# Stage A's stores on ScalarE's queue, back tables ahead of the filter copies, less filler: the set-up of an FFT and gated-FFN kernel

**Chip, cores, metric.** One core of one Trainium2 chip. The metric is the device time of a whole execution in microseconds (us). The traces' spans, from the first to the last instruction, are mostly some 1.8 us shorter than these times.

## The reference, cut to what matters

```python
def _attn_ref(x, filt_r, filt_i):            # x: 8 x 3008 x 256, f32
    X = np.fft.rfft(x, axis=1)
    Y = X * (filt_r + 1j * filt_i)[None]     # filters: 1505 x 256
    return np.fft.irfft(Y, n=x.shape[1], axis=1)

def _moe_ref(x, w_gate, w_val, w_out):       # on 24064 x 256 rows, d_ff 1536
    return np.maximum(x @ w_gate, 0.0) * (x @ w_val) @ w_out
```

The transform of 3008 is done as 94 x 32 with matmuls. For batch 0 nothing can hide it: its x is loaded, multiplied by a 94-point matrix ("stage A", `psA`), stored to a scratch in DRAM (`Abuf`), read back in another layout (`at`), and only then goes through the second transform, the products with the filters, and the inverse. The other seven batches do this beside the gated FFN, which keeps TensorE busy for the rest of the time.

## The kernel before: the parts concerned

Stage A of one batch: 16 tiles `psA`, cast by ACT to `asb`, and one store to `Abuf` for every four (there are four such quarters `c`):

```python
def items_a(b):
    def one(c, j, st):
        ...
        nc.tensor.matmul(psA[0:NROW], WA, XF[c * NC2 // NX2][:, o:o + 512], start=True, stop=True)
        nc.scalar.copy(dst, psA[0:NROW])
        if j == 3:
            eng = nc.scalar if b and c > 1 else nc.sync
            eng.dma_start(_ap(Abuf[b], ...), st["asb"][:NROW])
```

The set-up (cut). `load_x` issues 15 loads on SP (SyncE), three for each group of columns; GpSimd (POOL) loads the filters once the first half of x has landed; `warm(n)` is n filler matmuls on `junk`, meant to keep TensorE's clock up:

```python
    load_x(0, nc.sync, ((0, 0, q), (0, q, 2 * q), (0, 2 * q, 4 * q), (1, 0, 2 * q), (1, 2 * q, 4 * q)))
    nc.sync.dma_start(WF, ...)
    ...
    hold_gpsimd(XF[0][:, 4 * q - 8:4 * q])       # a small cast on POOL that waits for x
    for _ in filters:                             # the other seven filter loads, on POOL's queue
        pass
    warm(11)
    for i, f in enumerate(items_a(0)):
        f()
        if i == 12:
            load_at(0, 0)                         # reads of Abuf, on SP
            load_at(0, 1)
    for c in range(2, 4):
        load_at(0, c)
    for half in range(2):
        for a in range(2):
            place_filter(0, a, half, nc.vector.tensor_copy)   # 32 x 3072 bf16 each
    for i in range(3):
        make_back_t(i)                            # PE, then DVE casts to I2t
    warm(6)
    place_filter(1, 0, 0, nc.vector.tensor_copy)
    for i in range(3):
        make_back_u(i)                            # PE from I2t, then ACT casts to I2u
    place_own()
    for a, half in ((1, 0), (0, 1), (1, 1)):
        place_filter(1, a, half, nc.vector.tensor_copy)
    place_nyq()
    for i in range(15):
        warm(2)
    load_x(1, nc.sync, ...)                       # batch 1
```

Of the kernel before, what the change touches and what calls it, by code (L numbers as in the profile page):

```python
# [35 lines left out]
def _ap(t, offset_elems, ap_list):  # L36
    return dataclasses.replace(
        t, offset=t.offset + offset_elems, ap=[list(p) for p in ap_list]
    )
# [81 lines left out]
def kernel(  # L121
# [10 lines left out]
    nc = tc.nc  # L132
# [66 lines left out]
    def make_back_u(q):  # L199

        psI = ps.tile([128, 8, 64], FP32, tag=fft_tag(), name="psI")
        nc.tensor.matmul(psI, swap, I2t[:, 8 * q:8 * q + 8, :], start=True, stop=True)
        nc.scalar.copy(I2u[:, 8 * q:8 * q + 8, :], psI)

    def place_own():

        for i, t in enumerate((I2t, I2u)):
            o = 192 + i * 128
            nc.vector.tensor_copy(t[64:, NG - 2:, :],
                                  tabs[64:, o:o + 128].rearrange("p (g n) -> p g n", g=2))  # L210
        nc.vector.tensor_copy(M1, tabs[:NROW, 448:])
# [21 lines left out]
    def place_filter(fi, a, half, copy):  # L233

        dst = FILT[fi][1]
        gs = slice(H * half, H * half + H)
        r = a * 64
        copy(dst[r + 32:r + 64, gs, :], dst[r:r + 32, gs, :])

    def place_nyq():  # L240
        for (src, dst), n in zip(FILT, nyq):
            nc.vector.tensor_copy(dst[96:97, NG - 1, :], n)
# [20 lines left out]
    def fft_tag(side=False):  # L263
        if side and turn.get("side"):
            return turn["side"]
        turn["i"] += 1
        return turn["tags"][turn["i"] % len(turn["tags"])]

    def items_a(b):

        def one(c, j, st):
            if j == 0:
                st["asb"] = sb.tile([128, NC2 * D], BF16, tag="asb", bufs=4, name="asb")
            psA = ps.tile([128, 512], FP32, tag=fft_tag(True), name="psA")
            o = (c * NC2 % NX2) * D + j * 512
            nc.tensor.matmul(psA[0:NROW], WA, XF[c * NC2 // NX2][:, o:o + 512],
                             start=True, stop=True)
            dst = st["asb"][:NROW, j * 512:(j + 1) * 512]
            nc.scalar.copy(dst, psA[0:NROW])
            if j == 3:  # L280
                eng = nc.scalar if b and c > 1 else nc.sync
                eng.dma_start(_ap(Abuf[b], c * NROW * NC2 * D, [[NC2 * D, NROW], [1, NC2 * D]]),
                                  st["asb"][:NROW])
        for c in range(N2 // NC2):
            st = {}
            for j in range(NC2 * D // 512):
                yield lambda c=c, j=j, st=st: one(c, j, st)
# [59 lines left out]
    def load_at(b, c):  # L347
        if c == 0:
            ats[b] = sb.tile([128, NG, D], BF16, tag="at", bufs=1, name="at")
        nc.sync.dma_start(ats[b][c:c + 125:4],  # L350
                          _ap(Abuf[b], c * NROW * NC2 * D, [[D, 32], [4 * NC2 * D, NG], [1, D]]))
# [164 lines left out]
    def warm(n, cols=512):  # L516

        psJ = ps.tile([128, 512], FP32, tag=fft_tag(True), name="psJ")
        for i in range(n):
            nc.tensor.matmul(psJ[:, :cols], junk[:, 0:128], junk[:, :cols], start=True, stop=True)  # L520
# [21 lines left out]
        pass  # L542

    warm(11)
    for i, f in enumerate(items_a(0)):
        f()
        if i == 12:
            load_at(0, 0)
            load_at(0, 1)
    for c in range(2, 4):  # L550
        load_at(0, c)
    for half in range(2):
        for a in range(2):
            place_filter(0, a, half, nc.vector.tensor_copy)
    for i in range(3):
        make_back_t(i)
    warm(6)
    place_filter(1, 0, 0, nc.vector.tensor_copy)
    for i in range(3):
        make_back_u(i)  # L560
    place_own()
    for a, half in ((1, 0), (0, 1), (1, 1)):
        place_filter(1, a, half, nc.vector.tensor_copy)
    place_nyq()
    for i in range(15):
        warm(2)
    load_x(1, nc.sync, ((0, 0, 2 * q), (0, 2 * q, 4 * q), (1, 0, 4 * q)))

# [118 lines left out]
```

## Time and profile before

| | time, us | span, us | TensorE busy | granted clock |
|---|---|---|---|---|
| before | 895.06 (894.41 to 895.76, 3 runs) | 894.9 in the first trace, of a run of 896.64 | 97% | 0.998 |

A busy share of 97% leaves 3% of idle time to win, and the filler besides, which counts as busy. So what counts is where TensorE is idle or runs filler. In this kernel that is the first 60 us. The lines that show it are in the prediction.

### The profile page before, as it was taken

What the parts mean: (1) busy time and instruction counts of PE and PEld (TensorE: products, weight loads), DVE (VectorE), ACT (ScalarE), POOL (GpSimd) and SP (SyncE); (2) the same over time, 40 slices, a digit from 0 to 9 for tenths busy, and PEclk for the clock granted to TensorE, in tenths of its full rate; (3) what the DMA queues carried; (4) which work ended last, traced back from release to release, by engine and by line L of the source; (5) the groups of instructions that cost most, each with busy time, mean ns of one, the idle gap of its engine ahead of it and who ended that gap; (6) DMA issues with size and microseconds to landing.
All of it is one profiled execution on the core that took longest, in us unless ns stands there. A gap on an engine that the chain in (4) does not pass through costs nothing.

```text
span 894.9 us, 19039 instructions
## 1 busy us (share of the span) xinstructions
PE 871.8 (97%) x7090; PEld 508.0 (57%) x7210; DVE 569.0 (64%) x873; ACT 499.4 (56%) x891; POOL 364.6 (41%) x361
## 2 busy tenths in 40 slices
PE   8899999999999999999999999999999999999997
PEld 2335555556556565556655565556655566666665
DVE  2737766577665776667765677657766577655553
ACT  4375565556555556555655565555565555555553
POOL 4350698038661386415672167802867000000001
PEclk9999999999999999999999999999999999999999
DMA  8997448534465335463365333763446512331111
GB/s 246 288 224 164 135 132 176 113 96 116 123 156 135 113 101 140 129 144 92 100 172 136 97 100 105 181 139 79 115 140 149 120 31 81 82 73 36 37 32 53
DMA packets 114099, 109.18 MB, mean 122 GB/s; under 512 B 20359, under 2 KB 98599, under 8 KB 113366
## 3 DMA queue, kind: packets, MB, share of 16 engines
q1 hardware_dynamic: 90294, 80.10, 34.8%
q0 software_dynamic: 22992, 26.41, 12.1%
q8 instruction: 57, 0.93, 0.5%
q10 hardware_dynamic: 720, 1.45, 0.4%
q14 instruction: 36, 0.29, 0.1%
HBM read 61.93 MB, written 49.81 MB: 125 GB/s over the span
## 4 chain that ended last, share of the span: by engine, by line
PE 85%; DVE 4%; ACT 4%; DMA 3%; issue 1%; POOL 1%; SPq 1%; POOLq 0%; ACTq 0%; DVEq 0%
PE psG L467 26%; PE psO L486 25%; PE psV L467 24%; DVE prod L472 3%; PE psF L323 3%; ACT vsb L470 3%; PE psD L394 2%; PE psX L364 2%; PE psY L451 2%; DMA at<-Abuf 1%; DMA Fti<-in_filt_i_dram 1%; PE psJ L520 1%; SPq L340 1%; ACT dsb L401 0%; DMA XF<-in_x_dram 0%
## 5 line engine op out<-in xcount | busy, mean ns | idle before, releaser
L472 DVE SCALAR_TENSOR_TENSOR prod<-psG,vsb 128x512 bf16<-128x512 f32 x564 | 388.8, 690 | 263.7 <-ACT vsb L470 257.8
L470 ACT CAST vsb<-psV 128x512 bf16<-128x512 f32 x564 | 332.1, 589 | 263.9 <-PE psV L467 180.3
L467 PE MATMUL psG<-yT,WgT 128*128 128x512 bf16 x1107 | 330.7, 379 | 6.9 <-DVE prod L472 0.8
L486 PE MATMUL psO<-WoT,prod 128*128 128x256 bf16 x2256 | 336.4, 273 | 1.1
L467 PE MATMUL psV<-yT,WvT 128*128 128x512 bf16 x1030 | 315.2, 380 | 0.8 <-ACT asb L330 0.5
L486 PEld LDWEIGHTS <-prod 128*128 128x128 bf16 x2256 | 220.6, 98 | 143.4
L467 PEld LDWEIGHTS <-WgT 128*128 128x128 bf16 x1128 | 110.0, 98 | 136.2 <-issue 3.3
L467 PEld LDWEIGHTS <-WvT 128*128 128x128 bf16 x1128 | 98.6, 98 | 41.8 <-issue 30.5
L258 POOL CAST scr<-prod 128x8 f32<-128x8 bf16 x24 | 4.6, 191 | 258.8 <-DVE prod L472 258.8
L509 POOL DMA_DIRECT2D out_dram<-osb x5 | 2.6, 536 | 195.9 <-ACT osb L499 195.9
L380 DVE TENSOR_TENSOR tt<-psX,Ftr 128x512 bf16<-128x512 f32 x96 | 65.0, 681 | 7.9 <-PE psX L364 7.9
L499 ACT COPY osb<-psO 128x512 f32<-128x512 f32 x92 | 53.9, 586 | 27.9 <-PE psO L486 27.3
L309 POOL TENSOR_TENSOR fold<-XP 128x1024 f32<-128x1024 f32 x24 | 56.5, 2356 | 20.5 <-PE psF L323 19.4
L380 DVE TENSOR_TENSOR uu<-psX,Fti 128x512 bf16<-128x512 f32 x89 | 60.4, 679 | 0.0
L401 ACT CAST dsb<-psD 128x512 bf16<-128x512 f32 x96 | 51.5, 589 | 12.1 <-PE psD L394 11.7
L296 POOL DMA_DIRECT2D XP<-in_x_dram x96 | 56.7, 596 | 3.2 <-PE psG L467 1.6
L310 POOL TENSOR_TENSOR XP<-XP 128x1024 f32<-128x1024 f32 x24 | 56.4, 2350 | 1.9
L330 ACT CAST asb<-psF 128x512 bf16<-128x512 f32 x48 | 25.8, 589 | 30.5 <-PE psF L323 30.5
L330 DVE CAST asb<-psF 128x512 bf16<-128x512 f32 x48 | 30.9, 686 | 18.6 <-PE psF L323 17.0
L456 ACT CAST yT<-psY 128x512 bf16<-128x512 f32 x47 | 27.6, 586 | 22.9 <-PE psY L451 22.7
L458 DVE CAST yT<-psY 128x512 bf16<-128x512 f32 x47 | 32.0, 680 | 9.8 <-PE psY L451 9.8
L451 PE MATMUL psY<-M,dC 96*128 96x94 bf16 (+18 forms) x604 | 37.5, 198 | 0.6 <-DMA dC<-Dbuf 0.5
(70 smaller groups left out, 494.0 us busy)
## 6 DMA issues: line engine op xcount, KB each, us to landing
at<-Abuf SPq DMA_DIRECT2D x32, 384.0 KB
dC<-Dbuf SPq DMA_DIRECT2D x64, 192.0 KB
XP<-in_x_dram POOLq DMA_DIRECT2D x48, 256.0 KB, 5.9
Dbuf<-dsb SPq DMA_DIRECT2D x23, 512.0 KB
XP<-in_x_dram POOLq DMA_DIRECT2D x96, 96.0 KB, 2.7
Abuf<-asb SPq DMA_DIRECT2D x96, 96.0 KB
out_dram<-osb SPq DMA_DIRECT2D x69, 94.0 KB
XF<-in_x_dram SPq DMA_DIRECT2D x15, 256.0 KB
```

The source lines that it names most:

```text
L296: nc.gpsimd.dma_start(xp[r:r + 24, 0:4:2, :], _ap(x, (b * N1 * N2 + o) * D, [[N2 * D, 24], [47 * N2 * D, 2], [1, 512]]))
L309: tt(t, xp[:, 0:2], xp[:, 2:4], op=ALU.add)
L310: tt(xp[:, 2:4], xp[:, 0:2], xp[:, 2:4], op=ALU.subtract)
L330: copy(asf[:, :, q, :], banks[q])
L380: nc.vector.tensor_tensor(p, psX, filt, op=ALU.mult)
L401: nc.scalar.copy(dsb[:, a, o:o + 2, :], psD[a])
L451: nc.tensor.matmul(psY[:, o:o + w], dCs[b, n2 // 8][:, n2 % 8, h * 128:(h + 1) * 128], M1[:, n1:n1 + w], start=True, stop=True)
L467: nc.tensor.matmul(pt[:, :W], w[:, h, ft * 128:(ft + 1) * 128], yt[:, h, :], start=(h == 0), stop=(h == 1))
L470: nc.scalar.copy(vsb, psV[:, :W])
L472: nc.vector.scalar_tensor_tensor(prod, in0=psG[:, :W], scalar=0.0, in1=vsb, op0=ALU.max, op1=ALU.mult)
L486: nc.tensor.matmul(psO[:, t % 2], prods[ft][:, t * 128:(t + 1) * 128], WoT[:, ft, :], start=(ft == 0), stop=(ft == NFT - 1))
L499: copy(osb[:, t0 % 2:t % 2 + 1], psO[:, t0 % 2:t % 2 + 1])
```

## The change

Its intent: store batch 0's stage A from a second hardware queue, so that SP does nothing but reads and each read goes out as soon as its store has landed; make the back tables right after stage A instead of behind the filter copies; give two of the eight filter copies to ACT; and cut the filler by 8 matmuls, as the wait that it pads should be shorter.

```diff
-                eng = nc.scalar if b and c > 1 else nc.sync
+                eng = nc.scalar if not b or c > 1 else nc.sync
@@
-    for i, f in enumerate(items_a(0)):
+    for f in items_a(0):
         f()
-        if i == 12:
-            load_at(0, 0)
-            load_at(0, 1)
-    for c in range(2, 4):
+    for c in range(4):
         load_at(0, c)
-    for half in range(2):
-        for a in range(2):
-            place_filter(0, a, half, nc.vector.tensor_copy)
     for i in range(3):
         make_back_t(i)
     warm(6)
-    place_filter(1, 0, 0, nc.vector.tensor_copy)
+    place_filter(0, 1, 0, nc.scalar.copy)
     for i in range(3):
         make_back_u(i)
+    for a, half in ((0, 0), (0, 1), (1, 1)):
+        place_filter(0, a, half, nc.vector.tensor_copy)
     place_own()
-    for a, half in ((1, 0), (0, 1), (1, 1)):
-        place_filter(1, a, half, nc.vector.tensor_copy)
+    for a, half, copy in ((1, 0, nc.scalar.copy), (0, 0, nc.vector.tensor_copy),
+                          (0, 1, nc.vector.tensor_copy), (1, 1, nc.vector.tensor_copy)):
+        place_filter(1, a, half, copy)
     place_nyq()
-    for i in range(15):
+    for i in range(11):
         warm(2)
```

## The prediction

> **What bounds the kernel now.** I read the page first. TensorE (PE) is busy 97% of an 894.9 us span at a granted clock of 0.998, so the steady part is bound by PE, and the change does not touch it: the diff ends at the first block of batch 0's transform. All that the change can win is idle or filler time of PE before that. I then read the chain that ended last over the first 110 us. Columns: start, length, what.
>
> ```profile
> 14.76 9.27 DMA Fti<-in_filt_i_dram
> 24.03 0.96 DVE Ftr L238
> 25.00 0.95 DVE Ftr L238
> 26.33 1.75 DVE I2t L197 x5
> 28.12 0.59 PE psI L202
> 28.71 7.53 PE psJ L520 x30
> 36.63 0.67 DVE tt L380
> ```
>
> The set-up is one chain: filters land, VectorE (DVE) copies them, only then makes the back tables I2t, PE makes the table I2u from them, runs 30 filler matmuls (psJ, dead work that keeps its clock up), and only then starts the transform whose first product is at 36.6. From there to the first steady matmul (PE psV at 61.64) the chain goes through products, casts, the Dbuf store and the dC read. Nothing of that is edited, so I take it to slide as a block.
>
> Is the filler what holds PE, or does it only pad a wait? The timeline of 22 to 36 us and just after:
>
> ```profile
> 23.22 1.47 PE L520 MATMUL psJ<-junk 128*128 128x512 bf16 x5
> 27.46 1.25 PE L202 MATMUL psI<-I2t,tabs 128*128 128x512 bf16 x2 [0.27 <-DVE I2t L197]
> 28.50 7.74 PE L520 MATMUL psJ<-junk 128*128 128x512 bf16 x30
> 32.82 0.21 DVE L242 COPY Fti<-nyq 1x256 bf16<-1x256 bf16 x1
> 35.16 0.18 POOL L258 CAST scr<-at 32x8 f32<-32x8 bf16 x1 [18.73 <-DMA at<-Abuf]
> 36.16 0.41 PE L364 MATMUL psX<-at,F 64*64 64x256 bf16 x8
> ```
>
> GpSimd's small cast waits for the last piece of `at` (batch 0 read back from Abuf), so `at` is there at 35.1. Filler ends about 36.2: it overshoots by 1.0 us. DVE has been done since 33.0, so it has 3.6 us of slack before its first product at 36.61. The next limit is therefore `at`. What it waits for is in SyncE's (SP) queue timeline and waits (total, times, longest):
>
> ```profile
> 13.35 6.78 SPq L282 DMA_DIRECT2D Abuf<-asb  x3
> 21.03 2.98 SPq L350 DMA_DIRECT2D at<-Abuf  x2
> 24.10 0.79 SPq L282 DMA_DIRECT2D Abuf<-asb  x1
> 26.32 5.84 SPq L350 DMA_DIRECT2D at<-Abuf  x2
> SPq L282 <- ACT asb L279: 9.0, 4, 3.0
> SPq L350 <- DMA Abuf<-asb: 8.5, 4, 4.6
> ```
>
> SP's instructions in time order inside those merged rows: stores at 13.35, 16.39, 19.82; reads at 21.03, 23.41; store at 24.10; reads at 26.32 and 31.59. Each waits in line[...]. In the packet records the 96 packets of store 0 (4096 B), issued at 13.35, run only from 17.6 to 20.4, once all of x is in (last 8192 B packet 17.56); store 3, issued at 24.1, runs 28.4 to 31.1 behind two reads (512 B packets). Read 3 then starts a fresh round trip: issued 31.59, packets 32.9 to 34.4, landed 35.1. Around 31.5 to 32.9 the DMA engines stand nearly idle (0.03 of their time between 32 and 33 in the packet records). But before, they are full, which the busy table by stretches shows (last columns: clock, DMA share, GB/s):
>
> ```profile
> 18.00:23.00 5.00, 5.00 (x53) 1.93 (x53) 0.95 (x1) 3.34 (x7) 0.00 (x0) 1.00 1.14 274
> 23.00:28.00 5.00, 2.57 (x27) 0.90 (x20) 4.87 (x9) 0.82 (x2) 0.00 (x0) 0.93 1.17 258
> 28.00:36.00 8.00, 7.92 (x32) 3.26 (x30) 4.80 (x10) 1.17 (x2) 0.54 (x2) 0.83 0.85 270
> ```
>
> So the set-up is limited by DMA throughput until about 31, then by one latency, then by 1 us of filler.
>
> [...]after 2.1 us idle the filler's first six matmuls are 0.43 us apart, then 0.213.
>
> **The change, part by part.**
> 1. *Stores on ACT's row.* Removes 4 issues from SP (0.3 to 0.8 us each) and puts them between ACT's casts. ACT casts 0.58 us out of each 0.86, so four casts leave 1.1 us to absorb one issue: about 0 on stage A. Store 0 can be issued at 11.7 rather than 13.35 and does not queue behind x; [...]it should run about 13 to 16.5 and land by 17. That delays x by at most its own 1.0 us of engine time.
> 2. *A wait that the diff does not show.* In the built program, DMA completion semaphores are shared in rotation. With store 0 now in the rotation before the last x loads, the last x load on SP waits for store 0's semaphore. So it goes out about 16.7 instead of 12.0, and its data are there about 20.0; the last quarter of stage A wanted them at 19.0. Cost: 0.5 to 1 us on stage A, whose end moves from 22.6 to about 23.4.
> 3. *The at chain.* Stores 1, 2, 3 issued at about 16.5, 20.3, 24.2. Each takes 1.2 us to its first packet (as read 3 did), 2 to 3 us to run when two other rows compete, and 0.6 us to be seen. Store 3 lands at 28 to 29.3; reads 0 to 2 are out by then. Read 3: 1.3 to first packet, 1.6 to run, 0.7 to land: `at` complete at 31.6 to 32.9. A check by throughput: from 17.5 on, stores (3.1), reads (5.6), what is left of x (0.8) and filters (7.7) are about 17 us of time per engine; at the 1.17 seen with two rows, 14.7 us, so 32.2 plus 0.7 landing. I take 32.5 against 35.1.
> 4. *Tables before filters on DVE.* The six I2t casts (2.08 us) follow stage A at once, 23.6 to 25.7, not at 25.99; PE's I2u matmuls end near 26 with no idle gap before, so the filler runs at full clock.
> 5. *Two copies to ACT.* ACT: Ftr about 25.0 to 27.7 (after store 3's issue), three I2u casts to 29.5, Fti when the filter has landed, to about 33. DVE loses two copies (1.9 us) but its own-table copies now wait for I2u at 29.5: 0.6, three Fti copies 2.9, two small ones 0.3, so DVE is free at 33.3. That is about where it was (33.0), but its 3.6 us of slack is gone.
> 6. *Filler.* 22 matmuls of 0.213 from 26.1, some waiting for I2u's banks: ends about 31.3. No longer a bound. By itself the cut is worth only the 1.0 us of overshoot.
>
> First product: the later of DVE free (33.3) and `at` + transform (32.5 + 0.2 + 0.4 = 33.1), so 33.4 against 36.61: 3.2 us. Carried to the end: 895.06 - 3.2 = about 891.9.
>
> **The rivals.**
> (a) *Transfers only trade places.* For it: DMA share is above 1.1 from 18 to 28 us, the bytes are unchanged[...]. Filters may land near 31 instead of 28.2; then ACT's Fti copy ends at 34 and the first imaginary product waits. Gain 1.5 to 2: 893.2. Against: the 1.4 us hole at 32 and the 1.0 of filler overshoot are real and go away.
> (b) *The shared semaphore, or ACT, hurts stage A more.* If store 0 lands only at 18.5, the last x load is there at 21.5, stage A ends 2 us later, and store 3 with it: gain 1 or nothing, 894 to 895.[...]
> (c) *All goes at latency speed.* [...]`at` is there at 31, DVE a little earlier than I think: 4.5 us, 890.5.
> (d) *The gain is eaten later*, by the Dbuf store and dC read (2.4 and 3.4 us of the chain near 53 to 59). They follow their producers, and loads of batch 1's x move forward too, so I give it little.
>
> **Range and chances.** (a) and (b) pull up, (c) down. I predict 891.9, with 890.2 to 894.0 for 8 in 10. Two per cent is 17.9 us, while everything before the first product is 36.6 us, all of it tied to DMA; no rival reaches that in either direction: 0.01 faster, 0.98 within, 0.01 slower.
>
> **What would show it.** Right: GpSimd's wait for `at` ends near 32.5; first psX near 32.7 and first tt near 33.4; first psV about 58.4; the small DMA hole before the last read gone; SP's last x load issued after store 0 lands, with a short PE wait for XF before the last quarter of stage A; ACT's 32x3072 copies at 2.7 us each; the steady rows (690 ns prod, 589 vsb) unchanged. Wrong: first tt after 35, DVE ended by a filter's DMA, or a first psV that moved less than the first tt did. If the time fell by more than 5 us, something else than the set-up changed.

What the prediction said of the hardware without a trace or run of this case is cut where marked. No term of its sum went with the cuts: first product at 33.4 (the later of 33.3 for DVE and 33.1 for `at` and its transform) against 36.61, so 895.06 - 3.2 = 891.9. The 2.7 us of part 5 for an ACT copy of 3072 columns: the trace before gives the same as an estimate (ACT took 0.586 us for 512 columns and 0.266 for 128, and the straight line through the two comes to 2.72 at 3072). How queues share the DMA engines, on which store 0's times in part 1 rest, was an estimate of mine. The 1.0 us in part 1 is an estimate too: the packet time of store 0 in the trace before, 1.02 us over 16 engines. A "row" is a DMA queue: q1 on the page is SP's, q10 ACT's, q0 GpSimd's.

## The result, and the profile after

| kernel | median, us | runs | ratio to before, 95% interval |
|---|---|---|---|
| before | 894.77 (894.41 to 895.76) | 4 | |
| changed | 899.23 (898.41 to 899.76) | 4 | 1.0047 (1.003 to 1.0065) |

A ratio is the mean time of one kernel's fast runs over the mean of the other's of the same rounds, so not quite the ratio of the medians. The changed kernel is slower by about 4 us, not faster by 3. It is "the same" at the 2% bar, but the sign is clear.

SP's queue timeline of the changed kernel answers to the one quoted for the kernel before. Columns: start, length, engine, line, what, count; a merged row holds the waits between its instructions.

```profile
1.95 16.01 SPq L176 DMA_DIRECT2D XF<-in_x_dram  x15
18.01 0.62 SPq L536 DMA_DIRECT2D WF<-dft_fold  x1
18.67 16.56 SPq L350 DMA_DIRECT2D at<-Abuf  x4
35.33 5.06 SPq L176 DMA_DIRECT2D XF<-in_x_dram  x8
```

The 15 loads of x now take until 18.0; before, the last of them was issued at 12.02. SP's waits (total, times, longest) name what held it:

```profile
SPq L350 <- DMA Abuf<-asb: 13.9, 3, 7.6
SPq L176 <- DMA Abuf<-asb: 6.1, 1, 6.1
```

The second line is new, and no such dependence is in the source: a load of x (L176) waits 6.1 us for a store to `Abuf`. The semaphore numbers in the packed trace show why. In the first 41 us of this trace the transfers of SP's and ACT's queues carry eight completion semaphores in rotation: 107, 109, 110, 111, 113, 114, 116 and 117. In the kernel before, store 0 stood on SP behind all of x. In the changed kernel loads 8 and 9 of x carry 110 and 113, and store 0, on ACT, has the 111 between them; load 15 is the eighth transfer after it and carries 111 again. Its issue waits for that number: store 0's last signal on it came at 17.48, and load 15 was issued at 17.50.

What that did to TensorE, from its timeline (in brackets: idle before, and what ended it):

```profile
12.19 7.08 PE L276 MATMUL psA<-XF,WA 128*96 128x512 f32 x16 [1.14 <-DMA XF<-in_x_dram]
24.55 5.45 PE L276 MATMUL psA<-XF,WA 128*96 128x512 f32 x8 [5.29 <-DMA XF<-in_x_dram]
```

Stage A's last quarter waits 5.29 us for that load (the "hole" below), and its eight matmuls then take 5.45 us: the granted clock had fallen to one half at 21.4 and came back at 28.2 (a "cold" clock). Stage A ends at 30.0; before, it ended at 22.6. The chain that ended last, over the first 70 us, is now this:

```profile
11.70 5.78 DMA Abuf<-asb
17.50 6.92 DMA XF<-in_x_dram
...
24.55 5.45 PE psA L276 x8
...
39.05 0.69 DVE tt L380
...
63.94 0.43 PE psV L467 x2
```

Store 0, then the last piece of x, then stage A: the transfer that was to be sped up stands ahead of everything. From stage A to the first product, left out above, the chain runs through DVE's tables and filter copies, which end at 39.02. The transform of `at` was ready at about 38.9 (psX to tt takes 0.44 us in e9), so the two tie; DVE's slack is gone, as part 5 said. What follows has moved with it:

```profile
31.06 2.75 ACT L238 COPY Ftr<-Ftr 32x3072 bf16<-32x3072 bf16 x1 [0.44 <-ACT asb L279]
32.66 4.91 PE L520 MATMUL psJ<-junk 128*128 128x512 bf16 x22
38.49 0.41 PE L364 MATMUL psX<-at,F 64*64 64x256 bf16 x8 [0.92 <-PE psJ L520]
38.52 0.18 POOL L258 CAST scr<-at 32x8 f32<-32x8 bf16 x1 [21.99 <-DMA at<-Abuf]
38.81 0.21 DVE L242 COPY Fti<-nyq 1x256 bf16<-1x256 bf16 x1
```

`at` is complete at 38.5 instead of 35.2, the filler is shorter and at full clock as intended (22 matmuls in 4.91 us), and first tt is at 39.05 instead of 36.61. From there to the first psV it takes some 25 us in both traces: that part slid as a block. Stage A ended 7.4 us late but `at` only 3.3, because over half of the delay was given back: store 3 was issued at 30.65 instead of 24.10, but read 3, which waits for it, could follow after 4.0 us instead of 7.5. Store 3's first packet came 0.8 us after its issue, with the DMA engines nearly idle, instead of 4.3. The traces differ by only 1.7 us in span and the timed runs by 4, because the first trace of the kernel before caught a long run (896.64 us, above all four timed ones); a second one settles that below.

### The profile page after: what moved, and what is told of

Same layout as the page of the kernel before. It is cut to its first block, busy times and chain, and to the rows that moved or that the text cites. A ratio compares the mean times of both kernels' runs of the same rounds, so it can differ in the third digit from the quotient of the medians.

```text
span 896.6 us, 19143 instructions
## 1 busy us (share of the span) xinstructions
PE 877.3 (98%) x7202; PEld 508.0 (57%) x7202; DVE 566.9 (63%) x871; ACT 504.6 (56%) x893; POOL 365.0 (41%) x361
## 3 DMA queue, kind: packets, MB, share of 16 engines
q1 hardware_dynamic: 89846, 78.52, 34.3%
## 4 chain that ended last, share of the span: by engine, by line
PE 90%; DMA 5%; DVE 1%; ACT 1%; POOL 0%; issue 0%; SPq 0%; DVEq 0%; ACTq 0%
PE psV L467 27%; PE psG L467 26%; PE psO L486 26%; PE psF L323 3%; PE psY L451 2%; PE psD L394 2%; DMA dC<-Dbuf 2%; PE psX L364 2%; PE psA L276 1%; DMA out_dram<-osb 1%; DMA XF<-in_x_dram 1%; DMA Dbuf<-dsb 1%; DMA Abuf<-asb 1%; PE psJ L520 1%; ACT dsb L401 0%
## 5 line engine op out<-in xcount | busy, mean ns | idle before, releaser
L467 PE MATMUL psV<-yT,WvT 128*128 128x512 bf16 x1128 | 336.4, 379 | 0.7 <-ACT asb L330 0.5
L467 PE MATMUL psG<-yT,WgT 128*128 128x512 bf16 x1128 | 335.3, 379 | 0.7 <-ACT dsb L401 0.3
L401 ACT CAST dsb<-psD 128x512 bf16<-128x512 f32 x96 | 51.5, 589 | 12.1 <-PE psD L394 11.7
L456 ACT CAST yT<-psY 128x512 bf16<-128x512 f32 x47 | 27.6, 586 | 23.9 <-PE psY L451 23.7
```

The source lines that it names most:

```text
L401: nc.scalar.copy(dsb[:, a, o:o + 2, :], psD[a])
L467: nc.tensor.matmul(pt[:, :W], w[:, h, ft * 128:(ft + 1) * 128], yt[:, h, :], start=(h == 0), stop=(h == 1))
```

## The experiments

All kernels gave correct results. In the table, "stage A end", "at" (GpSimd's cast that waits for it) and "tt" (first product) come from the profiled run of each.

| run | what | ratio to before (95%) | stage A end | at | tt | span |
|---|---|---|---|---|---|---|
| b2_before | before, again | - (one look) | 22.8 | 35.1 | 35.6 | 892.9 |
| a2_after | changed, again | 1.0033 (1.0021 to 1.0045) | 30.1 | 38.4 | 39.1 | 896.4 |
| e4_stores_only | before + stores on ACT | 1.0039 (1.0027 to 1.0051) | 29.9 | 37.7 | 39.6 | 896.8 |
| e3_stores_back | the change without that | 1.001 (0.9994 to 1.0027) | 23.3 | 35.8 | 36.4 | 895.4 |
| e1_store1_sp | changed, store 1 on SP | 1.0003 (0.9991 to 1.0015) | 23.6 | 34.8 | 35.2 | 893.2 |
| e9_store0_late | changed, store 0 one cast later | 0.9982 (0.9968 to 0.9995) | 22.6 | 34.6 | 35.0 | 892.9 |
| e9b_store0_late | the same again | 1.0 (0.9988 to 1.0012) | 23.0 | 34.5 | 35.1 | 893.9 |
| e2_warm_gap | changed, filler in the hole | 1.001 (0.9998 to 1.0022) | 29.0 | 37.4 | 38.1 | 895.3 |
| e5_hold_filters | changed, filters later | 1.0037 (1.002 to 1.0055) | 24.5 | 37.5 | 38.1 | 896.2 |
| e7_filler | e1, 36 filler matmuls | 0.999 (0.9978 to 1.0003) | 23.7 | 35.3 | 35.7 | 894.4 |
| e10_late_filler | e9, 36 filler matmuls | 0.998 (0.9968 to 0.9992) | 22.3 | 33.8 | 34.2 | 891.6 |
| e11_late_only | before + e9's stores only | 1.0004 (0.9992 to 1.0016) | 23.3 | 35.1 | 37.2 | 894.3 |

Theory A: the shared semaphore is the loss, with the cold clock after it. Theory B: three DMA queues only trade places. Theory C: ACT's longer queue and DVE's new order hold the first product.

### Break the shared wait: e1_store1_sp

```diff
-                eng = nc.scalar if not b or c > 1 else nc.sync
+                eng = nc.scalar if not b and c != 1 or c > 1 else nc.sync
```

> One edit to the changed kernel: store 1 goes back to SP's queue, which takes one transfer out between store 0 and the last load of x in the rotation of the 8 completion semaphores, so that load no longer waits for store 0. Theory A (the shared semaphore, the hole it opens on PE and the cold clock after it are the whole loss): the last x load is issued near 12.0 us instead of 17.5, no PE wait of 5.3 us inside stage A, stage A ends near 23 instead of 30.0, at is complete near 32.5, first tt near 33.4, and the time is 2.5 to 3.5 us below the kernel before (ratio near 0.9965). Theory B (three DMA rows only trade places, semaphore or not): stage A ends near 23 but at is complete at 35 or later; ratio 1.000 or above. Theory C (ACT's longer queue and DVE's new order are what hold the first product): stage A near 23, at near 33, but first tt after 35.5 and released by DVE or ACT; ratio 0.999 or above.

The last x load went out at 12.30, the hole was gone, stage A ended at 23.6, and the time went back to that of the kernel before. That points to the semaphore; this edit also takes a store off ACT, which e9 below does not. But the 2.5 to 3.5 us of gain that A also promised did not come: `at` was complete at 34.8, not 32.5. On that B was half right.

### Filler in the hole: e2_warm_gap

```diff
-    for f in items_a(0):
+    for i, f in enumerate(items_a(0)):
+        if i == 12:
+            warm(24)
         f()
```

> One edit to the changed kernel: 24 filler matmuls (5.1 us) ahead of the last quarter of stage A, where PE stands idle for 5.3 us. The wait for x stays. Theory A with its clock part: the last eight stage A matmuls are 0.43 us apart instead of 0.86 for the first four, stage A ends near 28.2 instead of 30.0, and the time falls 1.5 to 2 us below the changed kernel's (ratio to the kernel before near 1.003 where the changed kernel had 1.0047). If the clock is no part of the loss: the ends of stage A and of the run stay within 0.4 us of the changed kernel's (ratio 1.0047).

```profile
20.16 5.34 PE L520 MATMUL psJ<-junk 128*128 128x512 bf16 x24
25.35 3.64 PE L276 MATMUL psA<-XF,WA 128*96 128x512 f32 x8
```

The wait for x stayed (in this trace TensorE restarted 0.8 us later than in the changed kernel's), but the eight matmuls took 3.64 us instead of 5.45. So 1.8 us of stage A's delay is the clock that fell while TensorE stood idle. Stage A ended at 29.0, not at the expected 28.2, because of the later restart, and the first psV came 1.2 us sooner than in the changed kernel's first trace. The time fell by 2 to 3 us, to 1.001; its interval touches that of the changed kernel's second set, so the size is uncertain.

### The parts by themselves: e3_stores_back and e4_stores_only

The edits are the hunks of the diff above: e3 takes the first two back (queue and order of the reads) and keeps the rest, e4 has only those two.

> The change without its first part: stores and reads of at as in the kernel before (all on SP, reads 0 and 1 ahead of store 3), but tables first, two copies on ACT and less filler. Theory A: no wait between store 0 and x, stage A ends at 22.6 as before, at complete at 35.2 as before, first psX right after it at 35.4 because the filler is out of the way, so 0.7 to 1.0 us faster than before (ratio 0.999). Theory C: the copies on ACT delay the first product, ratio above 1.001.

> The kernel before with only the first part of the change (stores on ACT, all reads after them on SP), filter copies, tables and 30 filler matmuls as before. Theory A: the last x load waits for store 0 as in the changed kernel, PE hole of about 5 us, stage A ends near 30; with 8 more filler matmuls (1.7 us) the filler ends near 39.3 and the first tt is near 39.8, so the time is 0.5 to 1 us above the changed kernel's (ratio near 1.0055). Theory C: without ACT's copies it is faster than the changed kernel, ratio below 1.003. Theory B: between them.

```profile
24.54 5.34 PE L276 MATMUL psA<-XF,WA 128*96 128x512 f32 x8 [4.83 <-DMA XF<-in_x_dram]
```

This is e4: the same hole, the same cold matmuls, and 1.0039, within the range of the changed kernel's two ratios. These two hunks alone make the loss. The extra 0.5 to 1 us for its longer filler can't be told from noise.

e3 gained nothing, a miss of mine. Its trace, TensorE:

```profile
25.91 4.91 PE L520 MATMUL psJ<-junk 128*128 128x512 bf16 x22
35.73 0.64 PE L364 MATMUL psX<-at,F 64*64 64x256 bf16 x8 [4.91 <-DMA at<-Abuf]
```

The tables come early, the filler ends at 30.8, and TensorE then stands idle for 4.9 us until `at` is there. Making the tables sooner and cutting the filler only moved the idle time, and the first transform starts on a cold clock (0.64 us for eight matmuls, where the kernel before has 0.41).

### All stores on ACT, without the shared wait: e9_store0_late, twice

Store 0 is issued after the next cast, at 13.3 instead of 11.7. That was to put it three places further on in the rotation. In the first of the two traces no load of x waits for a store any more: the one wait of such a load for a DMA is 0.2 us, for an earlier x load.

```diff
+            if late:
+                late.pop()()                      # ahead of the j == 3 part, after the cast
             if j == 3:
                 eng = nc.scalar if not b or c > 1 else nc.sync
-                eng.dma_start(...)
+                store = lambda: eng.dma_start(...)
+                if not b and not c:
+                    late.append(store)
+                else:
+                    store()
```

> All four stores stay on ACT's queue as the change has them; only store 0 is issued one cast later (about 13.9 instead of 11.7 us). In the rotation of completion semaphores it then falls three places later, and the last x load waits for an earlier x load, not for store 0. Theory A (the shared semaphore is the loss): the last x load issued near 12.3, no hole over 1 us inside stage A, stage A ends near 23, ratio to the kernel before 0.998 to 1.001, as in the run with store 1 on SP. If putting all stores in ACT's queue is itself the loss: the hole or a late store 3 stays and the ratio is 1.003 or more. at complete near 34.5, because each store waits 3 to 4 us for its first packet, as in the run with store 1 on SP.

> The mended kernel (store 0 one cast later, all stores on ACT) once more. If the gain of its first rounds (0.9982) is real: 0.997 to 0.9995 again, no hole over 1 us in stage A, and 0.994 to 0.996 of the changed kernel's time in the same rounds. If that was chance: 0.9995 to 1.001.

TensorE's timeline in e9_store0_late:

```profile
12.11 10.51 PE L278 MATMUL psA<-XF,WA 128*96 128x512 f32 x24 [0.82 <-DMA XF<-in_x_dram]
34.60 0.41 PE L372 MATMUL psX<-at,F 64*64 64x256 bf16 x8 [4.41 <-DMA at<-Abuf]
```

The hole is gone with every store still on ACT: 24 matmuls in one run, as before. In the same rounds as the changed kernel, e9b has 895.65 mean against 898.65, so the whole loss of these rounds, 3 us, goes with a 1.6 us later issue of one store. Against the kernel before, the first set showed a gain and the second none. Together they show parity or a gain under 0.2%. `at` was complete at 34.6 and 34.5: the cured change brings it forward by some 0.6 us, not by 2.7.

### Why the last load took so long: e5_hold_filters

The wait for store 0 delayed the load's issue to 17.5, which I had foreseen within a microsecond. But in the packet records of the changed kernel its first packet moves only at 21.7, 4.2 us after the issue.

```diff
-    hold_gpsimd(XF[0][:, 4 * q - 8:4 * q])
+    hold_gpsimd(XF[1][:, 4 * q - 8:4 * q])
```

> The changed kernel, with GpSimd's seven remaining filter loads held until the last x load has landed instead of until the first half of x has. The shared semaphore stays. It tells why the last x load, issued at 17.5 us, moved its first packet only at 21.9. If other rows' work ahead of it in the DMA engines is the reason: its packets start 1.0 to 1.5 us after its issue, PE's hole is 1 to 2 us instead of 5.3, and stage A ends near 24. If a fresh issue simply takes that long: the hole stays 5 us and stage A ends near 30. The filters land 5 us or more later, so the first product is later too and the whole time is above the kernel before in either case (ratio 1.002 to 1.008).

The DMA queues over 17.5 to 21.0 us (packets, MB, share of 16 engines; q1 is SP's, q10 ACT's, q0 GpSimd's), first the changed kernel:

```profile
q0 software_dynamic: 618, 0.50, 106.3%
q10 hardware_dynamic: 24, 0.10, 7.3%
```

then the run with the filters held:

```profile
q1 hardware_dynamic: 411, 0.44, 41.7%
q10 hardware_dynamic: 112, 0.39, 41.3%
```

In the changed kernel the filters have the engines to themselves until 20.3: SP's queue moves nothing for 3.5 us though the load was issued at the start of that window, and ACT's store 1, issued at 16.48, has moved a quarter of its packets. With the filters out of the way the load's packets come 1.4 us after its issue, though store 1 is moving on ACT's queue, and the hole is small:

```profile
20.88 3.65 PE L276 MATMUL psA<-XF,WA 128*96 128x512 f32 x8 [1.36 <-DMA XF<-in_x_dram]
```

So the hole is a product of two things: the shared semaphore makes the load late by 5.5 us, and being late it arrives behind filter work, worth about 3 us (4.2 less 1.4), that it used to be ahead of. The kernel as a whole did not gain, as expected: the held filters now ran from 24.0 to 35.8 beside store 3, which was issued at 25.17, moved its first packet at 29.34 and let read 3 go only at 32.95, so `at` was complete at 37.5. A first product (uu) then waited another 0.57 us for ACT's copy of a late filter.

The same wait accounts for most of the missing gain in the cured kernels. From the packet records, time from a store's issue to its first packet on ACT's queue: 3.5, 3.6, 3.6 and 4.1 us in e9_store0_late with x or filters in flight; 0.8 for store 3 in the changed kernel and store 1 in e5, with the engines idle or about a fifth busy. Of the four in e9, only store 0 had no store ahead of it on its own queue; stores 1 to 3 were issued while the one before them had not ended, and began 0.4, 0.9 and 1.8 us after it. So for them the part of the other queues is not told apart. In the kernel before, store 3 took 4.3 us on SP's queue, behind two reads. A second queue did not shorten it. Whether the work ahead sits in the DMA engines or in what feeds them, no run here tells.

### Does the idle time before the transform cost? e7_filler and e10_late_filler

```diff
-    for i in range(11):
+    for i in range(18):
         warm(2)
```

on e1 and on e9.

> The run with store 1 on SP, with 36 filler matmuls instead of 22: there PE stood idle from 31.2 to 34.7 us and its clock fell to half for the first transform matmuls. If that cold clock costs: the filler ends near 34.2, the six narrow filler matmuls after the first psX take 0.83 instead of 1.28 us, and first psV comes 0.3 to 1 us after less time from psX (25.5 us in that run), ratio near 0.9995. If DVE's products set the pace there: psX to psV stays 25.5 and the ratio stays 1.0003.

> The mended kernel with 36 filler matmuls instead of 22, which end near 33.2 us, still ahead of the last part of at near 34.6. If an idle PE ahead of the first transform costs through its clock: 0.3 to 1 us below the mended kernel (ratio about 0.0007 lower). If the products on DVE set the pace: the same as the mended kernel within 0.3 us.

First transforms in e9b, whose TensorE had been idle for 3.85 us:

```profile
34.46 0.64 PE L372 MATMUL psX<-at,F 64*64 64x256 bf16 x8 [3.85 <-DMA at<-Abuf]
36.43 0.64 PE L372 MATMUL psX<-at,F 64*64 64x256 bf16 x8
```

and in e10, idle for 0.92:

```profile
33.79 0.41 PE L372 MATMUL psX<-at,F 64*64 64x256 bf16 x8 [0.92 <-PE psJ L528]
34.90 0.41 PE L372 MATMUL psX<-at,F 64*64 64x256 bf16 x8
```

e7 shows no gain that can be told from e1: the filler ended at 34.3, but psX to psV took 25.7 us against 25.5, and the intervals of 0.999 and 1.0003 overlap. For e9 and e10: with more filler the first two transforms are 1.1 us apart instead of 2.0. Most of that is hidden behind the products on DVE: from first psX to the first Dbuf store it takes 8.5 us in e10, e1, e7 and before, and 9.1 in e9b. So a cold clock there cost 0 to 0.6 us in these traces. In timed runs e10 is 1.8 us below e9b of the same rounds. Their traces differ by 2.3 us in span, of which 0.8 lies in stage A, which ended earlier in e10's and has nothing to do with filler; so what the filler is worth is not shown. e10 is the fastest kernel measured, at 0.998 of before, but it was timed in one set of rounds only, and e9's two sets show how far such sets lie apart.

### Parting the cured gain, and the spread: e11_late_only, b2_before, a2_after

e11 is the kernel before with e9's store hunk and the new order of reads alone.

> The kernel before with only the mended first part (stores on ACT, store 0 one cast later, reads after them): filter copies, tables and 30 filler matmuls as before. It parts the mended kernel's gain. If it comes from the stores alone: at complete near 34.6 and ratio near 0.9982. If the tables and the shorter filler are needed as well: the filler ends between 34.4 (clock warm) and 36.2 (cold), first psX 35 to 36.2, ratio 0.9995 to 1.000.

It did not gain either (1.0004): `at` is there at 35.1, but the 30 filler matmuls behind the late tables ended at 36.9 in this trace, eight of them on a cold clock (granted 0.5 for 3.41 us, after a longest idle gap of 1.62 us). In these traces each half waits for what the other would mend (e3 for `at`, e11 for filler); that both together gain isn't shown either.

> The kernel before once more, for a second trace of it: how far its set-up varies from run to run. Expected: at complete between 34 and 35.5, first tt between 35.4 and 36.7, first psV between 60.3 and 61.6, span 893 to 895.

> The changed kernel once more, in the same rounds as the mended ones. Every theory: ratio to the kernel before 1.003 to 1.006, PE's hole in stage A 4.5 to 6 us.

TensorE in the second trace of the kernel before:

```profile
27.82 6.64 PE L520 MATMUL psJ<-junk 128*128 128x512 bf16 x30
35.11 0.41 PE L364 MATMUL psX<-at,F 64*64 64x256 bf16 x8 [0.66 <-PE psJ L520]
```

The filler took 6.64 us here, not 7.74, and ended before `at` was there. The overshoot of 1 us that I read from the first trace is a matter of whether the clock falls, and is absent in this one: in the first trace the granted clock was 0.5 from 27.3 to 30.7, after an idle gap of 2.12 us; here the longest gap was 1.39 us and the clock stayed at 1.0. Its span is 892.9 (just under the 893 expected), so the changed kernel is 3.7 us longer than this trace and 1.7 longer than the first; the timed ratios of 1.0047 and 1.0033 (4.2 and 3.0 us) fit the mean of the kernel before, whose eleven spans in a2's rounds run from 893.1 to 894.7.

## Why the prediction was wrong, point by point

- **What bounds it.** Right that only the set-up moved; the 1 us of filler at its end came from one trace.
- **Part 1 (stores on ACT).** Right that they cost ACT nothing: its issues take 0.3 us and its casts kept their pace (0.86 us apart, 0.97 across an issue). Store 0 ran 14.3 to 17.2 and was seen at 17.5, against a predicted start at 13 and landing by 17. That on a second queue it "does not queue behind x" was hardly so in e9: there store 0, issued at 13.29, moved its first packet at 16.74, when all but the last few packets of x were out. Store 0 behind x in the trace before (first packet at 17.58, the last one of x done at 17.56) shows the order within SP's queue, but nothing of how two queues share the engines.
- **Part 2 (the hidden wait).** This is the step that failed. The mechanism was right: the last x load waits for store 0, was issued at 17.5 (predicted 16.7), and TensorE waits before the last quarter of stage A. The size was not: "its data are there about 20.0 ... Cost: 0.5 to 1 us on stage A". Measured: first packet at 21.7, TensorE restarted at 24.55, stage A ended 7.4 us late. Of that 5.3 us are the hole, 1.8 the half clock after it (e2), and the rest small changes. The term mis-sized is the time from issue to first packet: I took 1.2 us from read 3 of the kernel before (1.36 when read exactly), which ran when the engines stood idle; behind filters in flight it is 4.2 (e5 shows 1.4 without them). I left out the clock, though the prediction itself has the filler's first six matmuls 0.43 us apart instead of 0.213 after 2.1 us idle.
- **Rival (b)** named this path, and put it at a landing of 21.5 and 2 us of stage A; it was worth more than three times that. It was the right rival with the same wrong latency, and so it got too little weight and the range no room above the old time.
- **Part 3 (at at 32.5).** Wrong with the wait (38.5), and wrong without it: 33.8 to 35.3 in the runs without that wait (e1, e7, e9, e9b, e10, e11). Issue of store 3 was as predicted or earlier (23.3 to 24.2 against 24.2); the term mis-sized most is again the time to the first packet, in e9 4.1 us instead of 1.2. Read 3 added a little: 4.7 us from issue to `at` instead of 3.6. (A slip in the sum: by its own terms store 3 lands by 29.0 at the latest, not 29.3.)
- **Parts 4 to 6 (tables, copies, filler).** Right in size: I2t straight after stage A, ACT's copies 2.75 us (estimated 2.7), 22 filler matmuls in 4.91 us, and in e9 DVE free at 32.2 (predicted 33.3). They are no gain by themselves (e3), as nothing waits for them while `at` is late.
- **The slide as a block and the 2% bar.** Right: some 25 us from first tt to first psV in both.

## What to carry to other kernels

Before a transfer is moved to another queue, look in the trace or the built program at which completion semaphores it shares: here store 0, entering the rotation earlier, made an unrelated load go out 5.5 us late, and issuing it one cast (1.6 us) later ended that. Take the time from issue to first packet from a place in the trace where the DMA engines are as busy as they will be, not from a quiet one (here 4.2 us behind filters in flight, 1.36 in the quiet place). Where several parts each wait for another, time each part alone: here the stores by themselves lost all that was lost, and neither the cured stores nor the earlier tables gained alone.
